# Sorted block attention and a mixture of experts on one core: the first stage in written order, and four smaller edits

## The chip, the cores and the metric

The kernel runs on one core of a Trainium2 chip. The metric is the device time of one execution in microseconds (us), lower being better; of several runs the median is given. Engines are named as in the profile: PE (TensorE, matrix products), PEld (its weight loads), DVE (VectorE), ACT (ScalarE), POOL (GpSimd) and SP (the queue that only issues transfers).

## The reference

Two parts, the second fed by the first. `P` is a sort matrix of 8 x 8 for each head, normalised by five rounds over rows and columns; it mixes the eight blocks of k and of v, and attention then runs within each block of 96 tokens. The result, 3072 tokens of 512 features, goes through eight experts, each weighted by a routing matrix that is itself normalised in eight rounds over all tokens.

```python
B, H, S, D = 4, 8, 768, 64        # 32 heads, 8 blocks of 96 tokens
for _ in range(5):                # P = sort_net
    P = exp(P - max(P, -1));  P /= sum(P, -1) + 1e-9;  P /= sum(P, -2) + 1e-9
k_sorted, v_sorted = P mixes the blocks of k, of v
scores = scale * q_b @ k_sb.T     # per block
attn = exp(scores - max);  attn /= sum(attn) + 1e-9
x = (attn @ v_sb) as (3072, 512)
G = exp(x @ w_gate - max)
for _ in range(8):
    G /= G.sum(1) + 1e-9;  G /= G.sum(0) + 1e-9;  G *= N / E
out = sum over e of G[:, e] * (relu(x @ w1[e]) @ w2[e])   # 512 -> 1024 -> 512
```

## The kernel before

The program is one straight list of instructions for each engine. It is written in a tile language: pools hand out buffers, waits are drawn from what each instruction reads and writes, and unless told otherwise a scheduler, which plays the program through with estimated costs, chooses the order in which the instructions stand on each engine. On the chip every engine takes its list strictly in that order.

**Loads.** Heads are loaded in pairs. `load_pair` (L61) issues three transfers from GpSimd's queue, k, v and q, each cast to bf16 on the way, into the pool `rawp`, which holds three pairs. Each of 128 partitions gets six consecutive tokens (CL) of two heads, so a block of 96 tokens lies on 16 partitions (CH). `relayout` (L72) copies q into `qq` and v into `kv` on GpSimd; `relayout_k` (L84) copies k into the other halves of `kv` on DVE (L87). `kv` and `qq` have two buffers each.

**Sort matrix.** The five rounds run on 32 partitions on DVE and ACT (L121 to L128). Eight small matmuls with `Ex` spread the result, and `build_R` (L245) multiplies it by a mask into the matrices `R`, for the first four heads on DVE and for the others on GpSimd, four heads at a time.

**One head g.** `q_transpose` (L259), once for a pair: six transposes on PE from `qq` into a psF buffer, then one copy of 64x768 on DVE for the first head and one on ACT for the second, which also put the tokens into their order. `sort_kv` (L271): six matmuls of `kv` with `R` into a psB buffer give k and v of that head, sorted and transposed; ACT casts them into `kvT_` (L280, three buffers), and SP issues a DMA transpose of the v half into `v1_` (L284, five buffers, whose column 64 holds ones). `scores` (L288): eight matmuls into psB, row maximum (L298) and subtraction (L300) on DVE, exp into `at_` on ACT (L302). `a_transpose` (L305): eight transposes into psF, copied into `aT_` by ACT (L310). `attend` (L312): eight matmuls with `v1_` into the only psO buffer; column 64 is the row sum, to which DVE adds EPS (L319), then takes the reciprocal (L320) and normalises into `og_` (L321). `x_transpose` (L326), once for a pair: eight transposes into psF, copied by ACT into `xtT` (L332), the input of the experts.

**Steps.** A loop over `s` from 0 to 34 runs these for different heads: scores of head s, sort of s+1, transposes of s-1, attention of s-2, and for pairs the load, relayout and transposes. The weights of expert 0 are loaded in step 2 and those of expert 1 in step 14 (`load_expert`, w1 and w2, 1024 KB each as bf16).

**Filling.** Expert 0 is cut into pieces: `l1_piece` (L165, four matmuls 128x384 and a relu on ACT, L174), `l2_piece` (L177, eight matmuls 128x512 and a copy on DVE, L184) and `gate_piece` (L187). When a quarter of the tokens is complete (heads 7, 15, 23), `add` puts the gate's and 22 such pieces into a list, and `fill`, called four times in each step, takes from it what an equal share of their estimated PE time allows. The last quarter runs between the eight rounds of the routing matrix, whose sums over tokens are one matmul with ones each (L404). All pieces, the transposes of q, of the weights `at_` and of `og_` use one PSUM pool, psF, with two buffers; psB has two and psO one.

**Experts 1 to 7.** For each chunk of 512 tokens 32 matmuls L424 with relus on ACT (L427), then 32 matmuls L437, which DVE adds to the output (L439). In each expert the weights of the next are loaded into the other of two buffers.

Of the kernel before, what the change touches and what calls it, by code (L numbers as in the profile page):

```python
# [24 lines left out]
def kernel(  # L25
# [11 lines left out]
    nc = tc.nc  # L37
# [21 lines left out]
    raw_t, kr_t, kv_t, qq_t = {}, {}, {}, {}  # L59
# [12 lines left out]
    def relayout(n):  # L72
        kr, vr, qr = raw_t.pop(n)

        kv = iop.tile([128, 2, CL, 2, D], BF16, name="kv")

        qq = iop.tile([128, CL, 2, D], BF16, name="qq")
        nc.gpsimd.tensor_copy(qq, qr.rearrange("p h c d -> p c h d"))
        for e in range(2):
            nc.gpsimd.tensor_copy(kv[:, e, :, 1 - e, :], vr[:, e])  # L80
            kr_t[n, e] = (kv[:, e, :, e, :], kr[:, e])
        kv_t[n], qq_t[n] = kv, qq

    def relayout_k(n):  # L84
        for e in range(2):
            to, of = kr_t.pop((n, e))
            nc.vector.tensor_copy(to, of)  # L87
# [17 lines left out]
    nc.vector.memset(kvT_[:, :, :, 96:128], 0.0)  # L105
    v1_ = perp.tile([128, NVB, NB, 80], BF16)
    nc.vector.memset(v1_[:, :, :, 64:65], 1.0)
# [116 lines left out]

    actx = ExitStack()
# [26 lines left out]
    og_ = perp.tile([96, 2, NB, 128], BF16)  # L252

    at_ = perp.tile([96, 2, S + 32], BF16)
    aT_ = perp.tile([96, 2, S + 32], BF16)
    nc.vector.memset(at_[:, :, S:], 0.0)
    nc.vector.memset(aT_[:, :, S:], 0.0)

    def q_transpose(n):  # L259

        tq = psF.tile([128, CL, 128], BF16, name="psF")
        for cl in range(CL):
            nc.tensor.matmul(tq[:, cl, :], qq_t[n][:, cl].rearrange("p e d -> p (e d)"), Ibf,
                             is_transpose=True, start=True, stop=True)
        for e in range(2):
            r = slice(64 * e, 64 * e + 64)
            (nc.vector.tensor_copy if e == 0 else nc.scalar.copy)(  # L267
                qT_[r, n % 2, e, 0:S].rearrange("p (m l) -> p m l", l=CL),
                tq[r].rearrange("p l m -> p m l"))
# [18 lines left out]
    def scores(g):  # L288
# [12 lines left out]
        at = at_[:, g % 2]  # L301
        nc.scalar.activation(out=at[:, 0:S].rearrange("p (i c) -> p i c", c=BL), in_=ssb.rearrange("p a i c -> p (a i) c"),  # L302
                             func=AF.Exp, scale=scale)

    def a_transpose(g):  # L305
# [4 lines left out]
        nc.scalar.copy(aT_[:, g % 2, 0:S], ta[0:96].rearrange("p i c -> p (i c)"))  # L310
# [33 lines left out]
    for s in range(NH + 3):  # L344
        if 4 + 4 * s < NH:
            build_R(nc.gpsimd, Pb, 4 + 4 * s, 4)
# [6 lines left out]
        if s < NH:  # L353
            scores(s)
# [120 lines left out]
```

## Time and profile before

| | |
|---|---|
| time, median of 3 runs | 791.41 us (787.96 to 793.26) |
| the profiled execution: time, span | 791.51 us, 789.7 us |
| mean granted TensorE clock | 0.98 |
| PE busy | 747.9 us, 95% of the span |
| DVE busy | 294.1 us, 37% |
| ACT busy | 330.6 us, 42% |
| POOL busy | 85.4 us, 11% |
| DMA | 37.41 MB in 47088 packets |

How to read it: busy times are sums over the whole span, and the span has stages with different limits, so a stage is read by itself. Rows of groups give line, engine, operation, output and input tiles, shapes, count, then busy time and mean duration in ns, then how long the engine stood idle just before these instructions and what ended it. Rows of a timeline begin with the start from the beginning of the span and the duration, both in us. PE's busy time includes the time in which a result still runs through the array, so a busy PE is not always a full one. "Landing" is the time from the issue of a transfer to its last byte.

### The profile page before, as it was taken

The page shows a single profiled execution, that of the slowest core. Times are in us where ns is not written, and L with a number is a line of the kernel's source. Part 1 is how long each engine was busy: PE and PEld are TensorE (multiplying, and loading weights), DVE is VectorE, ACT ScalarE, POOL GpSimd, SP SyncE. Part 2 cuts the span into 40 slices and gives each one's busy share as a digit, 9 for nine tenths or more (in the row PEclk, how much of TensorE's full clock was granted, in tenths as well). Part 3 has the DMA queues.
Part 4 walks back from the last instruction along what each step waited for, and adds up shares of the span by engine and source line. Part 5 has one row for each costly group of instructions (what it writes and reads, how often), then busy time and mean ns, then how long its engine had stood idle before and what let it go on. Part 6 is the DMA issues. An engine that isn't in the chain of part 4 may idle for free.

```text
span 789.7 us, 10603 instructions
## 1 busy us (share of the span) xinstructions
PE 747.9 (95%) x4444; PEld 377.6 (48%) x4444; DVE 294.1 (37%) x539; ACT 330.6 (42%) x537; POOL 85.4 (11%) x126
## 2 busy tenths in 40 slices
PE   1669899999999999999999999999999999999997
PEld 1667566655444444444444444444444444444443
DVE  7976787856852213121221212122121212212121
ACT  2777777754233342423334242333424233342422
POOL 8944441000000000000000000000000000000000
PEclk9768999999999999999999999999999999999999
DMA  9999961100600060004200230015000600002122
GB/s 120 138 182 177 147 88 27 29 8 1 107 1 1 0 107 1 0 1 74 34 0 1 53 54 1 1 15 92 1 1 0 107 1 1 0 1 94 67 81 81
DMA packets 47088, 37.41 MB, mean 47 GB/s; under 512 B 19392, under 2 KB 39872, under 8 KB 47040
## 3 DMA queue, kind: packets, MB, share of 16 engines
q0 software_dynamic: 26128, 26.23, 22.4%
q1 hardware_dynamic: 20912, 10.50, 6.8%
q8 instruction: 35, 0.57, 0.3%
q14 instruction: 13, 0.11, 0.0%
HBM read 52.45 MB, written 6.29 MB: 74 GB/s over the span
## 4 chain that ended last, share of the span: by engine, by line
PE 83%; DMA 6%; DVE 5%; ACT 4%; issue 1%; POOL 1%; ACTq 0%; DVEq 0%; POOLq 0%
PE oacc L437 37%; PE hps L424 36%; PE psF L171 4%; PE psF L182 4%; DMA kr<-in_k_dram 3%; DMA v__111<-kvT__109 3%; ACT hTs L174 1%; ACT at__208 L302 1%; ACT kvT__109 L280 1%; DVE osbl L184 1%; PE psF L308 1%; ACT aT__209 L310 1%; ACT qT__113 L267 1%; PE psF L330 1%; PE psB L293 0%
## 5 line engine op out<-in xcount | busy, mean ns | idle before, releaser
L427 ACT ACTIVATE hTs<-hps 128x512 bf16<-128x512 f32 x336 | 200.5, 597 | 379.5 <-PE hps L424 379.5
L424 PE MATMUL hps<-xtT,w1e 128*128 128x512 bf16 x1344 | 298.2, 379 | 0.0
L437 PE MATMUL oacc<-w2e,hTs 128*128 128x512 bf16 x1344 | 296.9, 379 | 0.0
L439 DVE SCALAR_TENSOR_TENSOR osbl<-oacc,glog,osbl 128x512 f32<-128x512 f32 x168 | 126.1, 751 | 437.8 <-PE oacc L437 437.8
L437 PEld LDWEIGHTS <-hTs 128*128 128x128 bf16 x1344 | 131.5, 98 | 158.3
L424 PEld LDWEIGHTS <-w1e 128*128 128x128 bf16 x1344 | 131.4, 98 | 157.4
L148 POOL DMA_DIRECT2D w1e<-in_moe_w_dram x8 | 6.1, 763 | 434.7 <-PE hps L424 374.6
L171 PE MATMUL psF<-xtT,w1e 128*128 128x384 bf16 x256 | 49.4, 327 | 1.7 <-ACT hTs L174 1.2
L182 PE MATMUL psF<-w2e,hTs 128*128 128x512 bf16 x192 | 44.9, 378 | 1.1 <-ACT hTs L174 0.5
L174 ACT ACTIVATE hTs<-psF 128x384 bf16<-128x384 f32 x64 | 31.1, 493 | 20.0 <-PE psF L171 19.3
L171 PEld LDWEIGHTS <-w1e 128*128 128x128 bf16 x256 | 24.6, 98 | 17.8 <-issue 4.5
L298 DVE TENSOR_REDUCE mx<-psB 96x8 f32<-96x768 f32 x32 | 30.1, 940 | 6.8 <-PE psB L293 6.7
L300 DVE TENSOR_TENSOR ssb<-psB,mx 96x768 f32<-96x768 f32 x32 | 30.4, 950 | 1.3
L302 ACT ACTIVATE at__208<-ssb 96x768 bf16<-96x768 f32 x32 | 27.0, 843 | 8.6 <-DVE ssb L300 8.6
L310 ACT COPY aT__209<-psF 96x768 bf16<-96x768 bf16 x32 | 25.4, 793 | 12.1 <-PE psF L308 11.8
L293 PE MATMUL psB<-kvT__109,qT__113 128*128 128x96 bf16 x256 | 23.6, 223 | 6.9 <-ACT kvT__109 L280 4.6
L280 ACT CAST kvT__109<-psB 128x768 bf16<-128x768 f32 x32 | 25.6, 799 | 10.4 <-PE psB L277 5.6
L182 PEld LDWEIGHTS <-hTs 128*128 128x128 bf16 x192 | 18.5, 99 | 20.0 <-issue 1.5
L277 PE MATMUL psB<-R,kv 128*128 128x128 bf16 x192 | 20.4, 246 | 5.6 <-DVE ssb L300 5.2
L293 PEld LDWEIGHTS <-qT__113 128*128 128x128 bf16 x256 | 17.9, 108 | 10.9 <-issue 7.5
L321 DVE TENSOR_TENSOR og__207<-psO,den 96x512 bf16<-96x512 f32 x32 | 21.8, 681 | 0.5
L308 PE MATMUL psF<-Ibf,at__208 96*128 96x96 bf16 x256 | 18.6, 223 | 2.9 <-DVE osbl L184 1.6
(80 smaller groups left out, 320.2 us busy)
## 6 DMA issues: line engine op xcount, KB each, us to landing
w1e<-in_moe_w_dram POOLq DMA_DIRECT2D x8, 1024.0 KB, 8.8
w2e<-in_moe_w_dram POOLq DMA_DIRECT2D x8, 1024.0 KB, 8.7
out_dram<-osbl SPq DMA_DIRECT2D x24, 256.0 KB, 2.0
kr<-in_k_dram POOLq DMA_DIRECT2D x16, 192.0 KB, 6.7
vr<-in_v_dram POOLq DMA_DIRECT2D x16, 192.0 KB, 6.7
qr<-in_q_dram POOLq DMA_DIRECT2D x16, 192.0 KB, 7.9
v__111<-kvT__109 SPq DMA_TRANSPOSE x32, 4.9
P<-in_sort_net_dram SPq DMA_DIRECT2D x1, 8.0 KB, 1.6
```

The source lines that it names most:

```text
L171: nc.tensor.matmul(hps[:, 0:HC], w1t[0][:, kk, fb * 128:(fb + 1) * 128], xtT[:, kk, c * HC:(c + 1) * HC], start=(kk == 0), stop=(kk == 3))
L174: nc.scalar.activation(out=hT0[c][:, fb, 0:HC], in_=hps[:, 0:HC], func=AF.Relu)
L182: nc.tensor.matmul(oacc, hT0[c][:, fb, tt * 128:(tt + 1) * 128], w2t[0][:, fb, :], start=(fb == 0), stop=(fb == 7))
L280: nc.scalar.copy(kvT_[:, g % NKT, :, 0:96].rearrange("p i (l c) -> p i l c", c=CH), mkap(kvps, [kvps.ap[0], [CH, NB], [128, CL], [1, CH]]))
L293: nc.tensor.matmul(sps[:, i // 4, (i % 4) * 96:(i % 4 + 1) * 96], qT[:, i * BL:i * BL + 128], kvT[:, i, 0:96], start=True, stop=True)
L300: nc.vector.tensor_sub(ssb, s4, mkap(mx, [mx.ap[0], [4, 2], [1, 4], [0, 96]]))
L302: nc.scalar.activation(out=at[:, 0:S].rearrange("p (i c) -> p i c", c=BL), in_=ssb.rearrange("p a i c -> p (a i) c"), func=AF.Exp, scale=s ...
L310: nc.scalar.copy(aT_[:, g % 2, 0:S], ta[0:96].rearrange("p i c -> p (i c)"))
L424: nc.tensor.matmul(hps, w1e[:, kk, fb * 128:(fb + 1) * 128], xtT[:, kk, nc4 * 512:(nc4 + 1) * 512], start=(kk == 0), stop=(kk == 3))
L427: nc.scalar.activation(out=hTs[:, fb, :], in_=hps, func=AF.Relu)
L437: nc.tensor.matmul(oacc, hTs[:, fb, tt * 128:(tt + 1) * 128], w2e[:, fb, :], start=(fb == 0), stop=(fb == 7))
L439: nc.vector.scalar_tensor_tensor(out=osbl[:, t, :], in0=oacc, scalar=glog[:, t, e:e + 1], in1=osbl[:, t, :], op0=ALU.mult, op1=ALU.add)
```

## The change

There are five edits.

- `tc.manual_schedule()` is entered ahead of the pools of the attention stage and closed after the last piece of expert 0. Within it each engine's instructions stand in the order in which the program writes them. The built program shows this order on all engines, except that a few instructions of expert 1 stand between those of expert 0, as before. The loop body is rewritten for it, with `scores` split into `scores` and `weights` (the exp), and `attend` into `attend` and `normalise`. `build_R` on GpSimd makes two heads at a time; `load_pair` comes in odd steps after the pair's buffer is free; a quarter's pieces are added at the end of a step.
- q is transposed straight from the loaded tile: `q_transpose` takes columns of two tokens of one head at a time, and two copies of 64x384 on each of DVE and ACT put the halves in their place. Tokens stand in another order within a block then, and the copy into `xtT` puts them back. The loaded q stays in its buffer until this transpose; `qq` and its copy are gone.
- EPS comes from a 97th row: `aT_` has a row of ones and `v1_` a row of EPS in column 64, so the matmul adds it to the sum, and the addition L319 is gone.
- k is copied by GpSimd too, together with v in `relayout`.
- Three memsets (`at_`, `aT_`, the row of ones) stand in the written order, on DVE ahead of the first `build_R`.

The diff, with context cut:

```diff
@@ -56,7 +56,7 @@
 
     rawp = ctx.enter_context(tc.tile_pool(name="rawp", bufs=3))
     iop = ctx.enter_context(tc.tile_pool(name="iop", bufs=2))
-    raw_t, kr_t, kv_t, qq_t = {}, {}, {}, {}
+    raw_t, kv_t = {}, {}
 
     def load_pair(n):
         raw = []
@@ -70,21 +70,13 @@
         raw_t[n] = raw
 
     def relayout(n):
-        kr, vr, qr = raw_t.pop(n)
-
+
+        kr, vr, _ = raw_t[n]
         kv = iop.tile([128, 2, CL, 2, D], BF16, name="kv")
-
-        qq = iop.tile([128, CL, 2, D], BF16, name="qq")
-        nc.gpsimd.tensor_copy(qq, qr.rearrange("p h c d -> p c h d"))
         for e in range(2):
+            nc.gpsimd.tensor_copy(kv[:, e, :, e, :], kr[:, e])
             nc.gpsimd.tensor_copy(kv[:, e, :, 1 - e, :], vr[:, e])
-            kr_t[n, e] = (kv[:, e, :, e, :], kr[:, e])
-        kv_t[n], qq_t[n] = kv, qq
-
-    def relayout_k(n):
-        for e in range(2):
-            to, of = kr_t.pop((n, e))
-            nc.vector.tensor_copy(to, of)
+        kv_t[n] = kv
 
     load_pair(0)
     load_pair(1)
@@ -103,8 +95,10 @@
     NKT, NVB = 3, 5
     kvT_ = perp.tile([128, NKT, NB, 128], BF16)
     nc.vector.memset(kvT_[:, :, :, 96:128], 0.0)
+
     v1_ = perp.tile([128, NVB, NB, 80], BF16)
-    nc.vector.memset(v1_[:, :, :, 64:65], 1.0)
+    nc.vector.memset(v1_[0:96, :, :, 64:65], 1.0)
+    nc.vector.memset(v1_[96:128, :, :, 64:65], EPS)
 
     qT_ = perp.tile([128, 2, 2, S + 32], BF16)
     nc.vector.memset(qT_, 0.0)
@@ -222,6 +216,9 @@
             ahead[0] -= c
 
 
+
+    order = ExitStack()
+    order.enter_context(tc.manual_schedule())
     actx = ExitStack()
     psB = actx.enter_context(tc.tile_pool(name="psB", bufs=2, space=PSUM))
     psO = actx.enter_context(tc.tile_pool(name="psO", bufs=1, space=PSUM))
@@ -250,23 +247,29 @@
             op=ALU.mult)
 
     og_ = perp.tile([96, 2, NB, 128], BF16)
+    ssb_t, ops_t = {}, {}
 
     at_ = perp.tile([96, 2, S + 32], BF16)
-    aT_ = perp.tile([96, 2, S + 32], BF16)
+    aT_ = perp.tile([97, 2, S + 32], BF16)
     nc.vector.memset(at_[:, :, S:], 0.0)
-    nc.vector.memset(aT_[:, :, S:], 0.0)
+    nc.vector.memset(aT_[0:96, :, S:], 0.0)
+    nc.vector.memset(aT_[96:97], 1.0)
 
     def q_transpose(n):
 
-        tq = psF.tile([128, CL, 128], BF16, name="psF")
-        for cl in range(CL):
-            nc.tensor.matmul(tq[:, cl, :], qq_t[n][:, cl].rearrange("p e d -> p (e d)"), Ibf,
-                             is_transpose=True, start=True, stop=True)
+
+        qr = raw_t.pop(n)[2]
+        tq = psF.tile([128, 2, CL // 2, 128], BF16, name="psF")
         for e in range(2):
-            r = slice(64 * e, 64 * e + 64)
-            (nc.vector.tensor_copy if e == 0 else nc.scalar.copy)(
-                qT_[r, n % 2, e, 0:S].rearrange("p (m l) -> p m l", l=CL),
-                tq[r].rearrange("p l m -> p m l"))
+            for c in range(CL // 2):
+                nc.tensor.matmul(tq[:, e, c], qr[:, e, 2 * c:2 * c + 2].rearrange("p l d -> p (l d)"),
+                                 Ibf, is_transpose=True, start=True, stop=True)
+        for e in range(2):
+            to = qT_[64 * e:64 * e + 64, n % 2, e, 0:S].rearrange(
+                "p (i c l h) -> p l c i h", i=NB, l=2, h=CH)
+            for l in range(2):
+                (nc.vector.tensor_copy if l == e else nc.scalar.copy)(
+                    to[:, l], tq[64 * l:64 * l + 64, e].rearrange("p c (i h) -> p c i h", h=CH))
 
     def sort_kv(g):
 
@@ -298,8 +301,11 @@
         nc.vector.reduce_max(out=mx, in_=s4, axis=AX.X)
         ssb = sp.tile([96, 2, 4, 96], F32, name="ssb")
         nc.vector.tensor_sub(ssb, s4, mkap(mx, [mx.ap[0], [4, 2], [1, 4], [0, 96]]))
-        at = at_[:, g % 2]
-        nc.scalar.activation(out=at[:, 0:S].rearrange("p (i c) -> p i c", c=BL), in_=ssb.rearrange("p a i c -> p (a i) c"),
+        ssb_t[g] = ssb
+
+    def weights(g):
+        nc.scalar.activation(out=at_[:, g % 2, 0:S].rearrange("p (i c) -> p i c", c=BL),
+                             in_=ssb_t.pop(g).rearrange("p a i c -> p (a i) c"),
                              func=AF.Exp, scale=scale)
 
     def a_transpose(g):
@@ -307,17 +313,20 @@
         for i in range(NB):
             nc.tensor.matmul(ta[:, i, :], at_[:, g % 2, i * BL:i * BL + 128], Ibf[0:96, 0:96],
                              is_transpose=True, start=True, stop=True)
-        nc.scalar.copy(aT_[:, g % 2, 0:S], ta[0:96].rearrange("p i c -> p (i c)"))
+        nc.scalar.copy(aT_[0:96, g % 2, 0:S], ta[0:96].rearrange("p i c -> p (i c)"))
 
     def attend(g):
-        n, r0 = g // 2, 64 * (g % 2)
         ops_ = psO.tile([128, 2, 4, 128], F32, name="psO")
         for i in range(NB):
-            nc.tensor.matmul(ops_[:, i // 4, i % 4, 0:65], aT_[:, g % 2, i * BL:i * BL + 128],
-                             v1_[0:96, g % NVB, i, 0:65], start=True, stop=True)
+            nc.tensor.matmul(ops_[:, i // 4, i % 4, 0:65], aT_[0:97, g % 2, i * BL:i * BL + 128],
+                             v1_[0:97, g % NVB, i, 0:65], start=True, stop=True)
+        ops_t[g] = ops_
+
+    def normalise(g):
+        n, r0 = g // 2, 64 * (g % 2)
+        ops_ = ops_t.pop(g)
         den = sp.tile([96, 2, 4], F32, name="den")
-        nc.vector.tensor_scalar_add(den, ops_[0:96, :, :, 64], EPS)
-        nc.vector.reciprocal(out=den, in_=den)
+        nc.vector.reciprocal(out=den, in_=ops_[0:96, :, :, 64])
         nc.vector.tensor_mul(
             og_[:, n % 2, :, r0:r0 + 64].rearrange("p (a i) d -> p a i d", a=2),
             ops_[0:96, :, :, 0:64],
@@ -329,44 +338,48 @@
         for i in range(NB):
             nc.tensor.matmul(tx[:, i, :], og_[:, n % 2, i, :], Ibf[0:96, 0:96],
                              is_transpose=True, start=True, stop=True)
-        nc.scalar.copy(xtT[:, hp, b * S:(b + 1) * S], tx.rearrange("p i c -> p (i c)"))
-
-    relayout_k(0)
+
+        nc.scalar.copy(xtT[:, hp, b * S:(b + 1) * S].rearrange("p (i h l) -> p i h l", h=CH, l=CL),
+                       tx.rearrange("p i (l h) -> p i h l", h=CH))
+
     build_R(nc.vector, Pps, 0, 2)
     nc.vector.tensor_copy(Pb, Pps[:, 0:256].rearrange("p (i g) -> p i g", g=32))
-    build_R(nc.vector, Pb, 2, 2)
     q_transpose(0)
     sort_kv(0)
-    relayout_k(1)
+    build_R(nc.vector, Pb, 2, 2)
     load_pair(3)
     nc.gpsimd.dma_start(out=wg, in_=moe_w_gate.rearrange("(kk k) e -> k kk e", k=128))
     NP = NH // 2
     for s in range(NH + 3):
-        if 4 + 4 * s < NH:
-            build_R(nc.gpsimd, Pb, 4 + 4 * s, 4)
-        if s % 2 == 1 and s // 2 + 1 < NP:
-            q_transpose(s // 2 + 1)
+        if 4 + 2 * s < NH:
+            build_R(nc.gpsimd, Pb, 4 + 2 * s, 2)
+        if s < NH:
+            scores(s)
+        done = s - 3
+        if done >= 0 and done % 2 == 1:
+            x_transpose(done // 2)
+        fill()
+        if 0 <= s - 2 < NH:
+            attend(s - 2)
         fill()
         if s + 1 < NH:
             sort_kv(s + 1)
         fill()
-        if s < NH:
-            scores(s)
-        fill()
         if 0 <= s - 1 < NH:
             a_transpose(s - 1)
-        if s >= 3 and (s - 3) % 2 == 1:
-            x_transpose((s - 3) // 2)
-            if (s - 3) % 8 == 7 and s < NH:
-                add([(0.7, gate_piece((s - 3) // 8))] + batch_pieces((s - 3) // 8), 33)
+        if 0 <= s - 2 < NH:
+            normalise(s - 2)
+        if s % 2 == 0 and s // 2 + 1 < NP:
+            q_transpose(s // 2 + 1)
         fill()
-        if 0 <= s - 2 < NH:
-            attend(s - 2)
+        if s < NH:
+            weights(s)
         if s % 2 == 0 and s // 2 + 2 < NP:
             relayout(s // 2 + 2)
-            relayout_k(s // 2 + 2)
-            if s // 2 + 4 < NP:
-                load_pair(s // 2 + 4)
+        if s % 2 == 1 and s // 2 + 4 < NP:
+            load_pair(s // 2 + 4)
+        if done % 8 == 7 and 0 < done < NH - 1:
+            add([(0.7, gate_piece(done // 8))] + batch_pieces(done // 8), 33)
         if s in (2, 14):
             load_expert(s // 8)
     actx.close()
@@ -410,6 +423,7 @@
             op0=ALU.mult, op1=ALU.mult)
     while pieces:
         pieces.pop(0)[1]()
+    order.close()
 
 
     for e in range(1, E):
```

## The prediction

> **What bounds the kernel now.** I read the slices of the span first, then the span cut into five stages (by the starts of the first and the eleventh row maximum, the last one, and the point from which expert 1 runs evenly), then groups by shape, the waits of each stage, and the chain of waits.
>
> ```profile
> PE   1669899999999999999999999999999999999997
> DVE  7976787856852213121221212122121212212121
> PEclk9768999999999999999999999999999999999999
> DMA  9999961100600060004200230015000600002122
> ```
>
> The last three quarters are TensorE alone. DVE is near full and DMA full only in the first tenth or two.
>
> ```profile
> 0.00:17.20 17.20, 1.17 (x16) 1.12 (x17) 11.97 (x47) 3.69 (x8) 13.64 (x25) 1.00 0.88 122
> 17.20:58.50 41.30, 28.50 (x352) 25.68 (x351) 35.05 (x61) 30.62 (x39) 30.94 (x42) 0.70 1.26 156
> 58.50:162.60 104.10, 97.51 (x1117) 66.58 (x1117) 80.63 (x153) 79.46 (x124) 30.95 (x48) 0.97 0.67 92
> 162.60:211.30 48.70, 47.36 (x308) 24.40 (x308) 30.35 (x87) 20.98 (x39) 1.65 (x2) 1.00 0.20 34
> 211.30:789.70 578.40, 573.40 (x2658) 259.76 (x2657) 136.10 (x195) 195.84 (x329) 8.18 (x10) 1.00 0.15 31
> ```
>
> (Columns: stage, length, busy time of PE, PEld, DVE, ACT, POOL, granted clock, DMA share, GB/s.) The last stage is 578.4 us of 512-column matmuls back to back, 6.91 us for 32 in the chain of waits; the change leaves it alone. So all is decided in the first 211 us. Stage two is steps 0 to 9, attention alone, 3.85 us a step (38.5 us from the maximum of head 0 at 20.0 to that of head 10 at 58.5). Stage three is steps 10 to 30 with expert 0's matmuls as filling: 104.1/21 = 4.96 us a step. From the maximum of head 15 to that of 19, to 23 and to 27 it is 19.9 us each, four steps of a steady pattern. From head 11 to head 15 it took 24.2.
>
> ```profile
> L300 DVE TENSOR_TENSOR ssb<-psB,mx 96x768 f32<-96x768 f32 x32 | 30.4, 950 | 1.3
> L298 DVE TENSOR_REDUCE mx<-psB 96x8 f32<-96x768 f32 x32 | 30.1, 940 | 6.8 <-PE psB L293 6.7
> L280 ACT CAST kvT__109<-psB 128x768 bf16<-128x768 f32 x32 | 25.6, 799 | 10.4 <-PE psB L277 5.6 <-DMA v__111<-kvT__109 4.6
> L80 POOL COPY kv<-vr 128x384 bf16<-128x384 bf16 x32 | 16.0, 528 | 3.1 <-PE psB L277 2.9
> L267 DVE COPY qT__113<-psF 64x768 bf16<-64x768 bf16 x16 | 15.1, 944 | 1.2 <-PE psF L263 1.2
> L87 DVE COPY kv<-kr 128x384 bf16<-128x384 bf16 x32 | 12.7, 405 | 4.3 <-DMA kr<-in_k_dram 4.3
> L319 DVE TENSOR_SCALAR den<-psO 96x8 f32<-96x8 f32 x32 | 5.0, 156 | 15.4 <-PE psO L316 15.3
> ```
>
> DVE, two heads: 2 x (0.940 + 0.950 + 0.156 + 0.193 reciprocal + 0.681 normalising) + 0.944 + 2 x 0.405 = 7.6 us. Stage two ran at 7.7 for two: DVE bounds it, except where transfers do:
>
> ```profile
> ACT kvT__109 L280 <- DMA v__111<-kvT__109: 4.6, 4, 2.0
> DMA to landing us min/median/max: 2.6/4.9/13.5
> ```
>
> The first is a wait of stage two, the second the line for the 32 v transposes (L284). While expert 0's weights came in (issued at 29.0 and 29.8, landed at 42.5 and 49.6) a v transpose took 8 to 13.5 us, and the casts of heads 5 to 10 follow the landing of the transpose three heads earlier, mostly within 0.1 us: kvT_ has three buffers.
>
> The 24.2 us have their cause in the chain of waits and in DVE's timeline:
>
> ```profile
> 61.36 18.58 DMA kr<-in_k_dram
> 82.10 0.87 DVE mx L298
> ```
> ```profile
> 76.70 0.15 DVE L319 TENSOR_SCALAR den<-psO 96x8 f32<-96x8 f32 x1
> 80.06 0.27 DVE L87 COPY kv<-kr 128x384 bf16<-128x384 bf16 x1 [3.21 <-DMA kr<-in_k_dram]
> ```
>
> A pair issued behind expert 1's weights (57.9 and 58.7) landed late, and DVE stood with a k copy (L87) at its head, the maxima behind it.
>
> **The change, part by part.**
>
> *Start (to the first maximum, 20.0).* Before, two k copies stand in DVE's Sinkhorn chain at 4.8 (with 1.1 us of waiting for k; L122 began at 5.46, its exp was done at 3.93) and two more at 12.3 to 13.3: about 1.5 + 0.8 us go. Added on GpSimd are four k copies, minus two q copies. L124 took 0.495 instead of 0.212 and L127 0.556 instead of 0.258 when GpSimd's kv copies ran beside them, 0.3 for two copies, so 0.6 for four more. On "who interferes with whom", the Trainium skill (SBUF — State Buffer) says that a VectorE instruction with two SBUF inputs and a GpSimd one that reads SBUF exclude each other for a whole instruction. The two slowed rows agree. By it all eight copies could each block once for 0.53, which would make the sum about 1 us worse; L300, with one input in PSUM, would stay free, as its steady 950 ns says. Also added is the memset of the 97th row, written ahead of build_R in DVE's order: 1600 bf16 elements on one partition. By L110 (1600 words in 1.39) it is 1.4, by L107 (40 elements in 0.09) not under 0.1; I take 1.4, since the count is L110's. With two small memsets 1.6, less the 0.46 in which the eight Ex matmuls run: +1.1. Sum -2.3 + 0.6 + 1.1, and 0.4 because no k copy stands ahead of the first maximum: -1.0 (bounds -2.4 to +1).
>
> *DVE per pair.* Gone are 2 x 0.405 and 2 x 0.156. q's copy becomes two of 64x384 on DVE and two on ACT. Between 512 columns at 0.681 and 768 at 0.944, 384 comes to 0.55 on DVE; ACT's 384-column relu is 0.49. So DVE 1.10 for 0.94, ACT 0.98 for 0.79. Per two heads DVE has 6.6 instead of 7.6: -0.5 a step where DVE is the bound. GpSimd has 64 x 0.53 = 33.9 instead of 30.7, in 211 us, with the R masks in halves; its 48 loads are issued as before, and nobody waits for it while three steps lie between a relayout and its sort.
>
> *Steps 0 to 9.* Five steps gain 0.5: -2.5. The other five run at the pace of the transposes. There the written order puts attend(s-2), which needs the same landing, before sort(s+1) on TensorE: three steps now take landing + 1.65 (attend, sort, cast) instead of + 0.87, 0.26 a step: up to +1.3, less where fewer transposes in flight land sooner; I take +1.0. Pair 5 is now issued behind expert 0's weights. The pair behind them before landed 1.7 to 4.3 us after them, so pair 5 lands near 50, about when q_transpose(5) stands on TensorE in step 8; 0 to 3, I take 0.5. The pairs issued behind it have more time. Sum -1.0 (bounds -5 to +4).
>
> *The stall behind expert 1's weights.* They move from 57.9 to step 14, near 76. No k copy is on DVE any more. Pair 11, next in the queue, has until step 18 (some 15 us) before GpSimd waits for it and until step 20 before TensorE does; a load in this position took 19 to 20. So -4.3 (24.2 - 19.9); at worst 0.
>
> *Steps 10 to 30.* Everything stays, the order becomes fixed. For four steps (eight first-layer pieces, three second-layer ones): PE 6.1 for attention (matmul columns x 0.422 ns, from 6.91 us for 32 x 512) and 10.7 for pieces, 17.2 with the gate's share; DVE 15 to 16.5; ACT 17.2 by durations, but back-to-back ACT instructions start 0.11 before the last one's end (129.84, 130.52, 131.21 in the timeline, for durations of 0.80 and 0.82), so 14.4. None fills 19.9. What binds is psF: two buffers through which every piece, aT, q and x must pass. I laid out one period by hand in the written order: four matmuls of a first-layer piece 0.65, eight of a second-layer one 1.73, 0.32 to 0.34 for six or eight of attention, 0.2 until ACT or DVE can start, 0.05 from a copy's end to the next user of its buffer. With the exp of one ACT-heavy step (four relus, x, q) ending at 0, the following exps end at 3.9, 9.1, 14.5 and 20.4. In the steps with two second-layer pieces TensorE waits for DVE's copies and ACT idles; in the ACT-heavy step TensorE waits for relus. So 20.4 for 19.9: +0.5 x 5.2 = +2.6. Bounds: with 18.4 (busiest engine 17.2, and 0.3 a step) -7.8; with nothing overlapped at ACT's ends, and attend waiting for the single psO, 21.4 to 22 by the same layout, +11.
>
> *Tail (162.6 to 211.3).* The same matmuls follow the last scores, 44.9 us by their columns, 47.4 busy of 48.7. The same Sinkhorn chain stands beside them: 0.
>
> Sum: -1.0 - 1.0 - 4.3 + 2.6 = -3.7 on a span of 789.7: 786.0. The profiled execution took 791.5 with 1.8 around its span, within 0.1 of the median 791.4. Forecast: **788 us**.
>
> **Rivals.** *A: the written order packs better than my layout.* Steps at 18.4 for four: 791.5 - 1 - 1 - 4.3 - 7.8 = 777. For: DVE is freed of 17.7 us (12.7 + 5.0), and PE is at 17.2 of 19.9. Against: DVE is not what the waits in stage three name; psF keeps its two buffers.
> *B: the psF ring in a fixed order.* Each attention transpose now stands between two pieces, and TensorE waits for an ACT copy queued behind a cast or an exp. At 22 for four steps +11: 791.5 - 6.3 + 11 = 796. It decides from 21.1 on (+6.3). For: the changed q copy holds its buffer for two copies on each engine, and TensorE cannot step aside. Against: back-to-back ACT instructions do overlap.
> *C: the transfers decide.* The stall comes back on TensorE as a q_transpose waiting for q behind either expert's weights; then the 4.3 are not gained: 792. For: landings of 19 to 20 us. Against: 15 us and more in hand.
>
> **Chances.** Forecast 0.42, A 0.25, B 0.23, C 0.10. One per cent, 7.9 us, is about what a measurement can tell here: faster than 783.5 is A and a little of the forecast, 0.28; slower than 799.3 the upper part of B, and a start and transfers worse than taken, 0.20; between, 0.52. The forecast's own range is 782 to 793; with A and B in it, 777 to 800.
>
> **What would show it.** First maximum near 19; heads 3 to 8 at 4 us or more a step with waits on the v transposes, now named by attend; no DVE wait for k near 80; four steps of the filling taking 20 to 21 us with TensorE waiting for copies from psF; gate and Sinkhorn as long as before. Wrong would be a period of under 19 or over 21.5 for four steps, or a wait of over 3 us for a load on TensorE.

## The result, and the profile after

The changed kernel takes 799.78 us (median of 4 runs, 798.99 to 800.88) where the kernel before takes 791.35 (787.96 to 793.26) in the same series: a ratio of 1.0112, 95% interval 1.0075 to 1.015. It is 1.1% slower; 788 was forecast. The profiled execution took 800.33 us, its span 798.4.

Two rows of slices, of the changed kernel:

```profile
PE   1778888899899999999999999999999999999997
DVE  7786666654862121312122121312122121212122
```

In the fourth to eighth slice PE now shows 8s throughout, where 9 8 9 9 9 stood: TensorE has gaps in the stage that was to keep its pace. The five stages of the changed kernel, cut at the first sort matmul, the maximum of head 10, that of head 31, expert 1's first second-layer matmul (columns as in the prediction; there the first cut was called the first row maximum, but 17.20 is the first sort matmul and the maximum of head 0 comes at 20.0):

```profile
0.00:17.50 17.50, 1.36 (x15) 1.15 (x16) 12.74 (x45) 3.69 (x8) 13.19 (x27) 1.00 0.91 124
17.50:57.10 39.60, 28.15 (x344) 24.90 (x343) 29.77 (x51) 31.17 (x45) 26.39 (x45) 0.74 1.11 147
57.10:169.50 112.40, 94.50 (x1124) 65.78 (x1125) 72.81 (x123) 81.89 (x135) 37.74 (x67) 0.98 0.64 89
169.50:220.80 51.30, 46.99 (x307) 24.30 (x306) 32.42 (x90) 20.29 (x39) 1.65 (x2) 1.00 0.15 24
220.80:798.40 577.60, 573.46 (x2657) 259.80 (x2655) 133.93 (x189) 196.43 (x329) 8.18 (x10) 1.00 0.16 32
```

The loss is in the third line, the filling: 112.4 us for 104.1. DVE's work there fell from 80.6 to 72.8 us, as the edits promised, and nothing came of it. TensorE is not busy in 112.4 - 94.5 = 17.9 us of it, where it was not in 104.1 - 97.5 = 6.6. (Its busy time is 3.0 us less for nearly the same matmuls, 1124 for 1117; so the idle time grows by more than the stage.) Cut at row maxima, the span of 798.4 differs from 789.7 in this way:

| stage | before | after | difference | forecast |
|---|---|---|---|---|
| to the maximum of head 0 | 20.0 | 20.8 | +0.8 | -1.0 |
| to that of head 10 | 38.5 | 36.3 | -2.2 | -1.0 |
| to that of head 31 | 104.1 | 112.4 | +8.3 | -4.3 + 2.6 = -1.7 |
| to expert 1's second layer (the tail) | 48.7 | 51.4 | +2.7 | 0 |
| the rest | 578.5 | 577.6 | -0.9 | 0 |

Groups of the changed kernel, by shape, that answer to those shown of before:

```profile
L303 DVE TENSOR_TENSOR ssb<-psB,mx 96x768 f32<-96x768 f32 x32 | 30.5, 954 | 2.2
L301 DVE TENSOR_REDUCE mx<-psB 96x8 f32<-96x768 f32 x32 | 30.4, 950 | 6.5 <-PE psB L296 6.1
L283 ACT CAST kvT__109<-psB 128x768 bf16<-128x768 f32 x32 | 25.4, 794 | 14.7 <-PE psB L280 14.4
L271 ACT COPY qT__114<-psF 64x384 bf16<-64x384 bf16 x32 | 15.1, 473 | 8.8 <-DVE qT__114 L271 8.5
L271 DVE COPY qT__114<-psF 64x384 bf16<-64x384 bf16 x32 | 11.3, 353 | 27.9 <-ACT qT__114 L271 16.8 <-PE psF L265 11.1
```

The durations are as before or better: q's copy on DVE is 0.353 us, where 0.55 was taken. The k copies and the addition of EPS are gone from DVE's list. New is what ends the idle time of L271: DVE waits 16.8 us for ACT's copies of the same tile and ACT 8.5 for DVE's. The line for the 32 v transposes is

```profile
DMA to landing us min/median/max: 2.7/3.8/10.3
```

so they land sooner (4.9 and 13.5 before), and the cast's 4.6 us of waiting for them (the ACT row of before) has no counterpart here: what idle time the cast has left is for the sort matmuls (L280). The chain that led through a late k is gone too. Where DVE stood 3.21 us for k, its timeline now has

```profile
81.33 0.34 DVE L271 COPY qT__114<-psF 64x384 bf16<-64x384 bf16 x1
82.73 0.36 DVE L271 COPY qT__114<-psF 64x384 bf16<-64x384 bf16 x1 [1.06 <-ACT qT__114 L271]
```

a wait for ACT in its place. The waits of TensorE in the filling (engine, what it was about to use, whom it waited for, sum, times, longest), the four largest:

```profile
PE psF L339 <- DVE og__210 L330: 4.9, 5, 1.2
PE psF L165 <- ACT hTs L168: 4.7, 10, 0.6
...
PE psF L176 <- ACT aT__212 L316: 2.4, 4, 0.9
...
PE psF L165 <- ACT xtT L342: 1.8, 5, 0.4
```

In the kernel before, the two largest were

```profile
PE psF L308 <- DVE osbl L184: 1.6, 1, 1.6
...
PE psF L171 <- ACT hTs L174: 1.2, 4, 0.4
```

All nine such rows of the changed kernel come to 18.6 us; those of before came to 6.2. L339, the transpose of `og_`, waits for the normalising. Six of the others, 12.8 us, stand at a psF buffer that ACT has yet to empty; the last two come to 0.9.

### The profile page after: what moved, and what is told of

It is laid out like the page before. It is cut to its first block, busy times and chain, and to the rows that moved or that the text cites. A ratio compares the mean times of both kernels' runs of the same rounds, so it can differ in the third digit from the quotient of the medians.

```text
span 798.4 us, 10584 instructions
## 1 busy us (share of the span) xinstructions
PE 744.5 (93%) x4444; PEld 375.9 (47%) x4444; DVE 281.7 (35%) x493; ACT 333.5 (42%) x553; POOL 87.1 (11%) x149
## 4 chain that ended last, share of the span: by engine, by line
PE 85%; DVE 8%; ACT 5%; issue 2%; ACTq 0%; DVEq 0%
PE oacc L451 36%; PE hps L438 36%; PE psF L176 4%; PE psF L165 3%; ACT qT__114 L271 1%; ACT kvT__109 L283 1%; ACT hTs L168 1%; PE psB L280 1%; DVE og__210 L330 1%; DVE ssb L303 1%; DVE mx L301 1%; PE psF L339 1%; DVE qT__114 L271 1%; PE psO L321 1%; PE psF L265 1%
## 5 line engine op out<-in xcount | busy, mean ns | idle before, releaser
L178 DVE COPY osbl<-psF 128x512 f32<-128x512 f32 x24 | 16.5, 688 | 20.3 <-PE psF L176 20.3
L77 POOL COPY kv<-kr 128x384 bf16<-128x384 bf16 x32 | 16.3, 510 | 64.8 <-PE psB L280 47.5
L314 PE MATMUL psF<-Ibf,at__211 96*128 96x96 bf16 x256 | 18.2, 220 | 5.5 <-ACT at__211 L307 4.2
L296 PE MATMUL psB<-kvT__109,qT__114 128*128 128x96 bf16 x256 | 18.6, 223 | 3.1 <-ACT kvT__109 L283 3.1
```

## The experiments

Theory 1: the written order costs the time; each engine stands at its next instruction where the scheduler had put one that could run. Theory 2: the new q copies cost it, four turns between two engines for one psF buffer. The ratio behind each time, with its 95% interval, is to the kernel before on the same chip. Stages are those of the profiled executions.

**e1, the scheduler back.** Only the written order is taken out; all edits and the rewritten loop stay.

```diff
-    order.enter_context(tc.manual_schedule())
```

> The changed kernel with the written order alone undone: the scheduler chooses again, from the changed loop; q straight from the loaded tile, EPS as a row and k on GpSimd stay. Theory 1 (the fixed order costs: an instruction that waits stands ahead of ready ones, above all DVE's normalising behind a copy of a second-layer piece): 785 to 792 us, and four steps of the filling under 20.5 us. Theory 2 (the q copies cost: they alternate between DVE and ACT, each waiting for the other, 1.85 us in which a psF buffer is held): the copies are still there, so 797 to 801.

Measured: 793.55 us (before 790.55; 1.0033, 1.0012 to 1.0054). The fixed order by itself costs 799.78 - 793.55 = 6.2 us: the filling takes 109.1 us for 112.4, the tail 48.8 for 51.4. The time lies between the ranges of the two theories, and four steps of the filling take 20.0 to 21.7 us from head 15 on, where theory 1 had under 20.5. So the rest is not faster than before either. What TensorE waits for in this filling is another thing than in the written order; the largest is

```profile
PE psB L295 <- ACT kvT__109 L282: 5.2, 10, 1.0
```

the scores waiting for the cast of the sorted k; 2.6 more go to one v transpose, and what stands at psF comes to 4.2.

**e2, all q copies on DVE.**

```diff
-                (nc.vector.tensor_copy if l == e else nc.scalar.copy)(
+                nc.vector.tensor_copy(
```

> The changed kernel with all four q copies of a pair on DVE, so that no copy waits for the other engine (about 1.4 us for the four instead of 1.85, and 0.96 less on ACT). Theory 2: some 7 us or more faster than the change, 790 to 793. Theory 1: 1 to 3 us faster, 797 to 799, and TensorE's waits for the normalised tile stay at 8 us and more.

Measured: 795.75 us (1.0058, 1.0038 to 1.0077), 4.0 less than the changed kernel. What was saved shows in the timeline of the changed kernel, at one q tile:

```profile
92.36 0.35 DVE L271 COPY qT__114<-psF 64x384 bf16<-64x384 bf16 x1 [1.77 <-PE psF L265]
...
92.74 0.96 ACT L271 COPY qT__114<-psF 64x384 bf16<-64x384 bf16 x2 [0.29 <-DVE qT__114 L271]
...
93.73 0.36 DVE L271 COPY qT__114<-psF 64x384 bf16<-64x384 bf16 x1 [1.02 <-ACT qT__114 L271]
```

The copies run in turns, 1.73 us from the first to the end of the last, and in the 1.02 us between its own two DVE stands with a row maximum next in its list. (The scores of this maximum were done at 93.65 and it began at 94.12, so here 0.5 us were lost.) Four copies on DVE alone are 4 x 0.353 = 1.4 us without a hand-over. Of the gain 1.4 us lie ahead of the first maximum, 1.8 in the steps to head 10, and 1.4 in the filling (111.0 for 112.4; by spans, 793.9 for 798.4). But 0.7 of the first 1.4 are not the copies': in this execution the rounds of the sort matrix, which come before any q copy, ended at 13.9 instead of 14.6. The time lies between the two expectations. Theory 2 holds for at most 4 us, not for all, and for little of the 8.3 in the filling; theory 1's sign is there, TensorE's waits for the normalised tile stay (5.1 us in the filling, 4.9 in the changed kernel).

The turns themselves are not new. In the kernel before a tile of q went

```profile
20.88 0.94 DVE L267 COPY qT__113<-psF 64x768 bf16<-64x768 bf16 x1
...
21.91 0.79 ACT L267 COPY qT__113<-psF 64x768 bf16<-64x768 bf16 x1
```

and at all 16 tiles ACT's copy begins behind the end of DVE's, at the closest 0.04 us behind it. In e4, where these two copies stand in the written order, they take 1.76 to 1.78 us at every tile. So four copies hold the psF buffer no longer than two did; new is that DVE has a turn at either end and stands in between.

**e3, the normalising right behind attend.** In the changed loop `normalise(s - 2)` stands behind the transposes of the weights, two stretches of filling after `attend(s - 2)`.

```diff
             attend(s - 2)
+            normalise(s - 2)
         fill()
...
-        if 0 <= s - 2 < NH:
-            normalise(s - 2)
```

> The changed kernel with normalise(s-2) written right after attend(s-2), ahead of the fill that can bring a second-layer piece. Theory 1: DVE no longer holds the normalising behind a copy that waits for TensorE; TensorE's wait for the normalised tile (8.4 us at the transposes into xtT) goes, 792 to 796. Theory 2: 799 to 801.

Measured: 797.42 us (1.0082, 1.006 to 1.0103), 2.4 less, between the two expectations. In the changed kernel the normalising came in this way, DVE held by a piece's copy:

```profile
97.42 0.69 DVE L178 COPY osbl<-psF 128x512 f32<-128x512 f32 x1 [1.35 <-PE psF L176]
...
98.03 0.19 DVE L329 RECIPROCAL den<-psO 96x8 f32<-96x8 f32 x1
98.26 0.69 DVE L330 TENSOR_TENSOR og__210<-psO,den 96x512 bf16<-96x512 f32 x1
...
99.00 0.51 PE L339 MATMUL psF<-Ibf,og__210 96*128 96x96 bf16 x8 [0.94 <-DVE og__210 L330]
```

attend had ended at 95.32, and psO was ready 2.7 us ahead of the reciprocal. In e3 TensorE's wait in the filling is

```profile
PE psF L339 <- DVE og__210 L330: 1.2, 1, 1.2
```

1.2 for 4.9. Of 3.7 us less waiting there only 1.1 arrive as a shorter filling (111.3 us for 112.4); the tail has 0.9 more of the gain.

**e4, the written order and its loop alone.** q, k and EPS as before, with the changed loop and the fixed order. The edit puts back `qq`, `relayout_k`, the addition of EPS and the old `q_transpose`:

```diff
+        nc.gpsimd.tensor_copy(qq, qr.rearrange("p h c d -> p c h d"))
-            nc.gpsimd.tensor_copy(kv[:, e, :, e, :], kr[:, e])
...
+        nc.vector.tensor_scalar_add(den, ops_[0:96, :, :, 64], EPS)
...
+            relayout_k(s // 2 + 2)
```

> The written order alone: the changed loop and the fixed order, with q, k and EPS as in the kernel before (q copied by GpSimd, k by DVE, the addition on DVE). Theory 1: slower still than the change, since DVE has 17.7 us more, 800 to 808. Theory 2: 788 to 795, since the q copies are two of full size again.

Measured: 802.76 us (1.015, 1.0132 to 1.0168), 12.2 us slower than before, in theory 1's range. The rewritten loop and the fixed order together are the largest effect of any part, and the small edits together take some of it back. The filling takes 114.5 us. At the start it is the other way: its first maximum is at 18.2, 1.8 us earlier than before and 2.6 earlier than in the changed kernel.

**e5, k and EPS alone.** The loop of before and its scheduler; k is copied by GpSimd, EPS comes from the 97th row.

```diff
+            nc.gpsimd.tensor_copy(kv[:, e, :, e, :], kr[:, e])
-            relayout_k(s // 2 + 2)
...
-        nc.vector.tensor_scalar_add(den, ops_[0:96, :, :, 64], EPS)
```

> The kernel before, its loop and its scheduler, with k copied by GpSimd and EPS as the 97th row, and nothing else. Both theories: DVE has 17.7 us less and no copy that waits for k at its head, so the stall near 80 us (4.3 us) goes: 784 to 789. If these two edits cost, by GpSimd's copies slowing the sort matrix or by the scheduler's other choices: 791 or more.

Measured: 784.95 us (before 790.67; 0.9928, 0.9908 to 0.9948). These two edits are worth 5.7 us, as forecast by both theories, and this version beats both kernels. The stage to head 10 falls from 38.5 to 32.5; four steps behind expert 1's weights take 21.6 instead of 24.2. But the filling as a whole takes 103.4 us for 104.1: the gain lies almost all ahead of it.

**e6, q direct alone.** The loop of before and its scheduler; only q is transposed from the loaded tile.

```diff
+        qr = raw_t.pop(n)[2]
+        tq = psF.tile([128, 2, CL // 2, 128], BF16, name="psF")
...
+            for l in range(2):
+                (nc.vector.tensor_copy if l == e else nc.scalar.copy)(
```

> The kernel before, its loop and its scheduler, with q transposed straight from the loaded tile and four copies, and nothing else. Theory 2 (these copies, alternating between the engines, are what the small edits cost): 794 to 798. Theory 1 (only the order costs): 790 to 792.

Measured: 793.87 us (1.0044, 1.003 to 1.0057), +3.2, nearly in theory 2's range. The stage to head 10 grows from 38.5 to 43.9 us, the filling falls from 104.1 to 99.1, in part because eight second-layer matmuls of expert 0 are left to the tail, which takes 50.9 for 48.7. The waits of this kernel from 20.1 to 64 us:

```profile
POOL qr L65 <- PE psF L264: 12.0, 3, 6.4
PE psB L295 <- ACT kvT__105 L282: 11.8, 6, 5.4
ACT kvT__105 L282 <- DMA v__107<-kvT__105: 10.1, 3, 5.1
```

A load into q's buffer now waits on GpSimd's queue for the transpose (first row), and the scheduler orders that queue anew: expert 0's w1 is issued at 14.95 (before 29.04) and expert 1's weights at 46.51 and 47.27 (before 57.90 and 58.66). So both land while the steps without filling run, where the cast waits for the v transposes (third row) and the scores for the cast (second row). The same edit moved loads, and with them a wait, from one stage to another.

**e7, the mends together.** The changed kernel with e2, e3 and the three memsets moved ahead of the sort matrix.

```diff
+    nc.vector.memset(aT_[96:97], 1.0)
...
-                (nc.vector.tensor_copy if l == e else nc.scalar.copy)(
+                nc.vector.tensor_copy(
...
             attend(s - 2)
+            normalise(s - 2)
```

> The changed kernel with three mends at once: all q copies on DVE, normalise right after attend, the three memsets ahead of the sort matrix. Theory 1 and theory 2 together: 4.0 and 2.4 us of the single mends and 1.2 for the memsets add up, 791 to 793. If the two waits cover each other: 794 to 796.

Measured: 793.41 us (1.0028, 1.0017 to 1.0039), 6.4 less than the changed kernel: 4.0 and 2.4 add up (793.4 lies just outside the range given for this), and the memsets add nothing that can be seen. In the trace the long one now stands ahead of the rounds (at 4.15, 1.39 us) and these end at 16.2 instead of 14.6: it was moved, not hidden. The written order can be mended to the scheduler's level with this loop (e1, 793.55), not to that of the kernel before.

**e8, a third psF buffer in the written order.** psO is cut to half its size to make room, with 64 columns for 65: the row sums are left out, the reciprocal reads ones in their place, and the output is not normalised. The first products of experts 1 to 7 have two buffers instead of three. The rest of the program is the changed kernel.

```diff
-    psF = ctx.enter_context(tc.tile_pool(name="psF", bufs=2, space=PSUM))
+    psF = ctx.enter_context(tc.tile_pool(name="psF", bufs=3, space=PSUM))
...
-        ops_ = psO.tile([128, 2, 4, 128], F32, name="psO")
+        ops_ = psO.tile([128, 2, 4, 64], F32, name="psO")
...
-    hpp = ctx.enter_context(tc.tile_pool(name="hpp", bufs=3, space=PSUM))
+    hpp = ctx.enter_context(tc.tile_pool(name="hpp", bufs=2, space=PSUM))
```

> The changed kernel with three psF buffers instead of two. The room comes from psO, which is one bank instead of two since the row sums are left out (the reciprocal reads ones, so the output is not normalised), and from one buffer less for expert 1 to 7's first products. If the two psF buffers are what a fixed order suffers from: the filling stage (row maximum of head 10 to that of head 31, 112.4 us in the change) falls to 104 or less. If waits on values rather than buffers decide: 109 to 113.

Measured: 786.67 us (0.994, 0.9926 to 0.9955), 13.1 less than the changed kernel with the same order and the same instructions but one column in 65 and what the reciprocal reads. The filling, and two of its waits:

```profile
56.00:153.90 97.90, 91.29 (x1124) 64.71 (x1125) 72.56 (x123) 80.53 (x135) 37.02 (x65) 0.97 0.73 100
```
```profile
PE psF L339 <- DVE og__210 L330: 5.1, 6, 0.9
PE psF L165 <- ACT hTs L168: 0.9, 3, 0.3
```

97.9 us for 112.4, as expected if the buffers bind, with TensorE idle in 6.6 of them instead of 17.9. The wait for the normalising is as long as ever, so the reciprocal that no longer reads psO has not shortened it. TensorE's waits at psF for ACT, 12.8 us in the changed kernel and 4.7 of them for the relus, are down to the 0.9 of the second row. The smaller buffer for experts 1 to 7 did not help: behind the tail the kernel takes 579.3 us for 577.6.

**e9, the same in the kernel before.** The same cut of psO and the third buffer, with the scheduler of before.

```diff
-    psF = ctx.enter_context(tc.tile_pool(name="psF", bufs=2, space=PSUM))
+    psF = ctx.enter_context(tc.tile_pool(name="psF", bufs=3, space=PSUM))
```

> The kernel before with three psF buffers, made as in the run with three buffers in the written order (no row sums, so the output is not normalised; one buffer less for experts 1 to 7). If two psF buffers bind any order of this stage: some 13 us or more faster, 777 or less, filling stage under 92 us. If it is the fixed order above all that suffers from them: at most 6 us faster, 784 to 790.

Measured: 782.84 us (before 790.41; 0.9895, 0.9861 to 0.9928), -7.6, between the two expectations. Its filling also takes 97.9 us, but not with the same work: 170 first-layer matmuls fall into it for 160 in e8, and its tail takes 44.4 us for 50.1. The two stages together take 142.2 us here and 148.0 in e8; with two buffers it is 152.8 and 163.7. So the two buffers bind either way, and the changed kernel pays more for them. But with three buffers it still stands 786.67 - 782.84 = 3.8 us behind, which the third buffer does not take away; the largest wait left in e8 is that for the normalising.

**e10, the three small edits in the loop of before,** with its scheduler: e5 and e6 together.

> The three small edits (q direct with its four copies, EPS as a row, k on GpSimd) in the loop of the kernel before, under its scheduler. If the effects add: 790.6 - 5.7 + 3.2 = 788. The scheduler with the changed loop took 793.6; if the edits spoil each other rather than the loop: 792 to 795.

Measured: 786.5 us (0.9953, 0.9935 to 0.9971), -3.9, a little better than the sum. q direct costs 786.5 - 784.95 = 1.5 us on top of k and EPS, where it cost 3.2 alone; but the intervals of e5 and e10 overlap. And the step from here to e1, 793.55 - 786.5 = 7.0 us, is the rewritten loop, with the scheduler in both.

**e11, e10 with all q copies on DVE.** The edit is that of e2.

> The same three small edits in the loop before, with all four q copies on DVE. Theory 2 (the alternating copies are q's cost): 782 to 785, at or under the 785 of k and EPS alone. If DVE then is too full, 786 to 789.

Measured: 785.26 us (0.9936, 0.9912 to 0.996). The time lies just outside theory 2's range, and the interval of e10 overlaps it; where the scheduler can put other work into the gap, the turns of the q copies cost about 1 us at most, for 4.0 in the written order.

**e12, the loads and pieces of the rewritten loop.** e10 with three things the rewritten loop moves: loads at the end of odd steps, R for two heads at a time, a quarter's pieces added at a step's end.

```diff
-        if 4 + 4 * s < NH:
-            build_R(nc.gpsimd, Pb, 4 + 4 * s, 4)
+        if 4 + 2 * s < NH:
+            build_R(nc.gpsimd, Pb, 4 + 2 * s, 2)
...
-            if s // 2 + 4 < NP:
-                load_pair(s // 2 + 4)
+        if s % 2 == 1 and s // 2 + 4 < NP:
+            load_pair(s // 2 + 4)
```

> The three small edits in the order of before, chosen by the scheduler (786.5 us as measured alone), with what else the rewritten loop moves apart from attention itself: pairs are loaded at the end of odd steps, R is made two heads at a time, and a quarter's pieces are added at the end of a step instead of in its middle. The rewritten loop under the scheduler took 793.55. If the loads and the filling's start cost these 7 us, this kernel takes 792 to 794. If it is the order of attention's own parts (scores first, then attend, sort, transposes of the weights, the normalising behind them), it stays at 785 to 788. In between, both have a share.

Measured: 789.52 us (before 790.46; 0.9987, 0.9974 to 1.0): between the two. Of the loop's 7.0 us these moves have 789.52 - 786.5 = 3.0; 793.55 - 789.52 = 4.0 are left for the order of attention's own parts. The filling takes 99.2 us in e10, 102.2 here and 109.1 in e1, but the pieces are shared out differently between it and the tail; the two stages together take 150.9, 153.0 and 158.0. Which of the three moves, and which part of attention, was not tried.

The parts, each as a difference of two runs: k and EPS -5.7, q direct +1.5, loads and pieces +3.0, attention's order in the loop +4.0, the order fixed +6.2. Together +9.0, where the changed kernel stands 8.4 to 9.2 above before (791.35 and 790.55). Each begins where the one ahead of it ended, so the sum comes out by construction and confirms nothing. They were taken on top of each other in this order only.

## Why the prediction was wrong, step by step

**What bounds the kernel.** Right for the last stage (577.6 for 578.4 us) and for psF as what binds the filling: e8 and e9 show it, 15.8 and 10.6 us of the filling and the tail together for one more buffer. Both runs also leave out the row sums and take a buffer from experts 1 to 7; in e8 the waits give no sign that either of these is the gain, and in e9 only the 0.8 us that TensorE had waited for psO are gone too.

**Start: -1.0 forecast, +0.8 measured.** Three terms, each a little short. The rounds of the sort matrix end at 14.6 instead of 15.6: -1.1, for -1.7. From there to the first product with the mask it is +1.4, for +1.1, and from there to the maximum +0.4, for -0.4. Of the 0.6 that the first is short, 0.4 is there ahead of the rounds: `v1_` takes two memsets now, and that of `qT_` behind them begins at 2.31 instead of 1.92, a term that the prediction did not have. The slowing of the rounds by GpSimd's copies, taken as 0.6 more, came to 0.7 more: the five products of each kind (L118, L121) took 1.3 us longer than their shortest in sum, where before it was 0.6. (Eight copies that each block once for 0.53 would be 4.2 us; the "about 1 us worse" that the prediction put for this does not come out of its figures.) The longest of them, and the second term, show in GpSimd's and DVE's timelines:

```profile
8.56 0.57 POOL L78 COPY kv<-vr 128x384 bf16<-128x384 bf16 x1
9.01 0.56 POOL L77 COPY kv<-kr 128x384 bf16<-128x384 bf16 x1
```
```profile
8.58 1.07 DVE L118 TENSOR_TENSOR P<-P,rs 32x64 f32<-32x64 f32 x1
...
15.62 1.39 DVE L256 MEMSET aT__212<- 1x1600 bf16 x1 [0.37 <-issue]
```

L118, 0.21 us when alone (at 13.53), was held through two GpSimd copies and ended at 9.65, just behind the second. The Trainium skill (SBUF — State Buffer, "Who interferes with whom") has the two kinds exclude each other for a whole instruction; the trace agrees, and shows that one can lose twice in a row. It is not so in every execution: in e2, the same program up to there, this product took 0.47. The memset of one partition took 1.39 us, for 1.4 taken. The third term is the q copies again:

```profile
18.09 0.97 ACT L271 COPY qT__114<-psF 64x384 bf16<-64x384 bf16 x2 [5.06 <-DVE qT__114 L271]
...
19.08 0.80 ACT L283 CAST kvT__109<-psB 128x768 bf16<-128x768 f32 x1
```

In the written order they stand ahead of the cast on ACT, and wait for DVE's first; the cast began at 18.06 before. With the q copies on DVE (e2) it begins at 17.66, 0.7 of the difference being the shorter rounds, and the first maximum comes at 19.35.

**Steps 0 to 9: -1.0 forecast, -2.2 measured.** Right in sign. The step priced at +1.0, attend ahead of sort at late transposes, hardly came: TensorE's wait for a v transpose before attend (L321) is 0.26 us, once, at 45.67, and heads 3 to 9 run at (52.38 - 28.51)/6 = 3.98 us a step.

**The stall behind expert 1's weights: right in kind, too large in size.** No engine waits for a load after 57 us. But four steps that were to fall from 24.2 to 19.9, -4.3, fell to 22.3, -1.9. TensorE's waits there are 3.9 us, 0.9 of them for the normalising and the rest at psF. And not all of the 4.3 was the stall's: in e5, with k off DVE and the order of before, the same steps take 21.6 with TensorE busy in 21.2; its granted clock is 0.72 in the first 5.4.

**Steps 10 to 30: the step that failed.** Four steps were taken at 20.4 us, +2.6 in all. From head 15 on they took 21.6, 20.4 and 23.2, mean 21.7 (before 19.9), 5.6 more in sum, and the last four before head 31 took 19.9 for 16.5, 3.4 more. One step more, from head 10 to 11, has 1.2. With the -1.9 above that is the +8.3. The prediction had said that over 21.5 would be wrong. Rival B, the psF ring in a fixed order, which was to decide from 21.1, is what happened; its 796 lacks the start and the tail and still has the whole 4.3 as gained. The failed term is the layout by hand, 20.4 us for four steps. Three things in it were too good:

- q's copies were taken as 1.10 on DVE beside 0.98 on ACT. They run in turns, 1.73 us, as the two copies of before already did (1.77 at the closest), which its trace showed. The Trainium skill (PSUM — Partial Sum Buffer, "PSUM bank collisions raise a hardware error") says that two engines must not be in one bank on the same 32 partitions at once; of the four copies the first and second read different halves, and by it could overlap. The trace has them one after the other all the same; what keeps them apart was not tried. e2: 1.4 us of the filling.
- The normalising was taken at the place of attend; the changed loop has it two stretches of filling later, and the transpose of `og_` waits in TensorE's list. e3: 1.1 us of the filling; with both mends (e7) it takes 108.4 us, 4.0 less.
- That a late copy holds one of two psF buffers, and that TensorE then cannot pass to anything else, was counted as 0.5 us a period. This is the rest, 108.4 for 104.1, by subtraction; in e7 TensorE's waits at psF for ACT still come to 8.8 us. With a third buffer (e8) the filling needs 97.9 us, with the first two points still in it.

That the order and its loop, not the new copies, are the main cause is shown by e4 and e10: with the old q, k and EPS they cost 12.2 us, and the small edits without them gain 3.9. Some 7 us of it come with the loop and not with the fixing: the scheduler does not undo what the loop asks for. By what mechanism the loop costs them under the scheduler stays open; e1's waits for the cast are a sign, not a proof.

**Tail: 0 forecast, +2.7 measured.** "The same matmuls, the same chain" left out that the order between them is fixed too. TensorE's rows of the rounds' sums (L417; three of six that waited):

```profile
197.95 0.39 PE L417 MATMUL csps<-cs,onesc 128*128 128x8 f32 x2 [1.00 <-DVE cs L415]
...
201.10 0.39 PE L417 MATMUL csps<-cs,onesc 128*128 128x8 f32 x2 [1.03 <-DVE cs L415]
...
213.99 0.39 PE L417 MATMUL csps<-cs,onesc 128*128 128x8 f32 x2 [0.64 <-DVE cs L415]
```

The six waits come to 3.8 us; in the kernel before, four came to 0.9, the longest

```profile
211.04 0.39 PE L404 MATMUL csps<-cs,onesc 128*128 128x8 f32 x2 [0.36 <-DVE cs L402]
```

The difference, 2.8, is as large as the 2.7. With the scheduler back (e1) four such waits come to 0.9 again, and the stage takes 48.8 us.

## What to carry to other kernels

An order written by hand must be priced by the buffers that everything passes through, not by the busy time of the engines: here, with two PSUM buffers, late copies stopped the engine that feeds them, and a lighter DVE bought nothing in that stage. Two copies out of one PSUM tile by two engines are in turns until the trace shows otherwise, so one engine that does all of them may be faster; the trace of the kernel before can be asked for this ahead of the change. A stage cut out of two kernels is compared only after counting what work falls into it. And edits that come in one package are worth measuring one by one: here two of five were worth 5.7 us, and the package lost 8.4.

## What the runs showed of the hardware that was not expected

- A DVE instruction with two SBUF inputs was held through two GpSimd copies in a row: 1.07 us for one of 0.21.
- DVE's copy of 64x384 bf16 from PSUM takes 0.353 us, where 0.55 had been drawn from the rows of 512 and 768 columns (0.681 and 0.944); ACT's takes 0.473.
- One more PSUM buffer of 2 KB a partition for the ring was worth 7.6 us to the kernel before and 13.1 to the changed one, in runs that leave out the row sums and take a buffer from experts 1 to 7.
- DVE's and ACT's copies out of different halves of one PSUM tile never overlapped, at 16 tiles of the kernel before and 16 of the changed one.
